# Local/global attention and a hard-swish layer on one core: all steps in a new written order

## The chip, the cores and the metric

The kernel runs on one core of a Trainium2 chip. The core has five instruction queues that run beside each other and wait for one another only through semaphores: TensorE (PE, with its weight loads PEld), VectorE (DVE), ScalarE (ACT), GpSimd (POOL) and SyncE (SP). SP issues most of the DMAs, POOL issues some. The metric is the device time of one execution in microseconds (us): 318.76 us is the median of three runs (317.52 to 319.28). A lower time is better.

## The reference

For each of 8 batches and 8 heads there are 512 local positions and 32 global ones, with a head size of 64. A global query attends to all 544 keys. A local query attends to the 32 global keys and to the local keys at a distance of at most 32. The result, 4352 rows of 512, goes through two dense layers with a hard-swish between them:

```
s_g  = scale * q_g @ [k_g, k_l].T ;  out_g = softmax(s_g) @ [v_g, v_l]
s_l  = scale * [q_l @ k_g.T, where(|i-j| <= 32, q_l @ k_l.T, -1e9)]
out_l = softmax(s_l) @ [v_g, v_l]
x = concat(out_g, out_l) per batch, heads side by side      # 4352 x 512
h = x @ w_in                                                # 512 -> 2048
y = (h * clip(h + 3, 0, 6) / 6) @ w_out                     # 2048 -> 512
```

## The kernel before

The kernel is straight-line: every step is a token in one long string, `ORDER`, and `run` calls a small function for each token. `pin` then chains the instructions of each engine (and the DMA issues of SP and POOL) in that written order. So the string fixes, for each of the five queues, which instruction stands behind which. It doesn't fix when one starts: that is set by the queue ahead of it and by the semaphores. A second string, `SEATS`, names for each tile that a token takes which physical buffer ("seat") it gets: 7 banks of PSUM (`ps`), 13 staging buffers for loads (`stg`), 3 or 4 buffers of each kind for the rest.

Work goes by pairs of heads, numbered p = 4 * batch + m, so 32 pairs in 8 batches, four pairs to a batch. The tokens that matter here, with the argument after the dot and often an engine letter at the end (v = VectorE, a = ScalarE, g = GpSimd, s = SyncE):

- `ld.p.c` loads k, q or v of a pair into a staging buffer (256 KB, on SP's queue); `lw.i.n` and `lw.o.n` load 16 blocks each of w_in and w_out the same way.
- `ca.p.c.e` casts a staged k, q or v to 16 bits; `cw.i.n.e` and `cw.o.n.e` cast a weight block. All casts and most copies go through the helper `copy`, L132.
- `Tp` and `Te` transpose a k or q on TensorE and copy it out of PSUM; `Td` does the same by a DMA transpose on SP's queue instead. `qw` copies 32 columns of a transposed q (the wrap of the window). `kg`, `vg`, `vG` and `vs` put the global keys and values and a shifted copy of the values beside the local ones.
- `Sp.p.ch` computes half of a pair's scores (8 half-height matmuls of 128 columns: four windows for each of two PSUM tiles), `Se` is the exponential on ScalarE (L295). The mask of the window is put in one of two ways: `Sm.p.ch` writes it into the PSUM tiles ahead of the scores by two matmuls of 512 columns (L273), or `Sv` multiplies the exponentials by zeros and ones on VectorE (L299).
- `Ap` multiplies the exponentials with the values (L332, L335), `An` divides by the row sum on VectorE (L344, L345), `Qp`, `Qe`, `Pp`, `Ga` and `Gv` do the global queries.
- `Xd` transposes a pair's result for the dense layers by DMA, `Xp` and `Xe` do it on TensorE with a copy.
- `Hp.f.c.m0.m1` are matmuls of the first dense layer for batch f and hidden block c (L409; f = 8 is the 256 global rows), `Ha` and `Hv` the hard-swish on ScalarE (L414) and VectorE (L420); `Hv` is also what frees the PSUM seat.
- `Op.f.t.c4` are four of the 16 matmuls of an output tile (L428), `Oe` copies it out, `Os` stores it from SP's or POOL's queue (L445).

Batches overlap by the written order: while TensorE does the second dense layer of one batch, the attention of the next is put in between in short bursts of scores. The first batch is special: nothing can fill TensorE until loads, casts and transposes of pairs 0 to 3 are through, and the w_in blocks arrive behind them.

Of the kernel before, what the change touches and what calls it, by code (L numbers as in the profile page):

```python
# [14 lines left out]
def kernel(  # L15
# [40 lines left out]
ps 00123456012341653064120645132054321506324062615302421206545230542654452541255146206153461236140236142305121050  # L56
25613024354613410320613456143562416451325434512034510264640621350432015042630631543265152431605431654321036456
01452301052164103461042563124561256130135650124564305216340252150421362530652433254625416520264351052463050216
531456405162351064326346365102345620562021564032351065624620316053405616341652314502601432650134065234514210 ;
stg 0123456789abc0123456798bc12304a65798c1b3042a65798c1b3042a657981cb3042a67c8594b302a617c89b4103265c7a489132056a4  # L60
b19728c3b46157cab349527 ;
kn 01230213021302103201233103230120 ;
qn 01230213021321302130123120313120 ;
qT 01231023102312302132103210232002 ;
E 01210210210210210210210201210210 ;
xn 01201201201202102102102102120121 ;
t1 01230120132103210321023103120312032130120120132013201321032103102310231203201320132013201323013202310231023102
1302130213012301231023102310231032 ;
ot 0123120132313213130013030122210202
# [10 lines left out]
    def const(name, shape, dtype=FP16):  # L80
        return constp.tile(shape, dtype, tag=name, name=name)
# [12 lines left out]
    vg = const("vg", [P, B, H, D])  # L94
# [423 lines left out]
iv id ig fg.1.v im fv.1.v ov.0.0 ov.0.1 ld.0.k lg.k.0 ca.0.k.a wm.7 Gc.k.0.a Gp.k.0 ld.0.q lv.0 Tp.0.k ld.1.q fv.0.v  # L518
ov.1.0 ov.0.2 ca.0.q.v Tp.0.q fk.0 Te.0.q.v Ge.k.0.a kg.0.v ld.1.k ld.2.q Te.0.k.a qw.0.v ld.2.k ld.3.k ld.2.v ld.3.q
ca.2.q.v fg.0.g ca.1.q.g Tp.1.q Te.1.q.a ca.2.k.a ca.1.k.g Tp.1.k qw.1.g Te.1.k.v vg.0.2.v Sp.0.1 Sp.1.0 Se.1.0.1 ik  # L520
Se.0.1.1 vg.0.0.v Sv.0.1.1 lw.i.6 ld.0.v ld.1.v Se.0.1.0 lw.i.5 Sp.1.1 lw.i.4 ld.3.v lw.i.0 lw.i.2 lw.i.7 lw.i.1
lw.i.11 lw.i.3 Se.1.1.1 lw.i.8 lw.i.10 vg.0.1.v ca.3.k.g lw.i.9 ld.4.q lw.i.12 lw.i.14 lg.k.1 lw.i.13 lw.i.15 lw.o.2
ld.4.k ld.5.q lw.o.0 lw.o.1 Tp.2.q Tp.2.k Se.1.0.0 Tp.3.k Te.2.q.a Te.2.k.a lw.o.3 Te.3.k.v lg.q.0 Sm.2.1 ca.2.v.v
ca.3.q.g qw.2.v Se.1.1.0 vs.2.v vg.0.3.v ca.1.v.g ca.0.v.v vs.0.g vs.1.g cw.i.4.g Sm.0.0 Sp.0.0 Se.0.0.0 Sp.2.1 Tp.3.q
Se.0.0.1 Sm.2.0 Sp.2.0 Sm.3.0 Se.2.1.0 Se.2.0.0 Se.2.1.1 ca.3.v.g Se.2.0.1 Sv.0.1.0 Sv.1.1.0 Te.3.q.v qw.3.v Sp.3.0
Ap.0.1 Ap.0.0 Se.3.0.0 ov.0.3 Sm.3.1 Sp.3.1 Sv.1.1.1 Sv.1.0.0 Sv.1.0.1 An.0.0 An.0.1 Ap.1.0 Ap.1.1 Se.3.1.1 fe.3
Se.3.1.0 An.1.0 Xp.0 Xe.0.a An.1.1 Ap.2.1 Ap.2.0 Xp.1 Se.3.0.1 Hp.0.4.0.1 An.2.0 An.2.1 Xe.1.a cw.i.0.g vs.3.g
Hp.0.5.0.1 fe.0 cw.i.5.a Ap.3.1 An.3.1 Ap.3.0 Hp.0.0.0.1 cw.i.2.a Xp.2 Hp.0.4.1.2 Hp.0.6.1.2 An.3.0 cw.i.11.g cw.i.6.v
Hp.0.2.0.1 Xe.2.a ca.4.q.g cw.i.1.v Xp.3 Hp.0.6.0.1 Gc.k.1.g Hp.0.0.2.3 Hp.0.4.2.3 Hp.0.5.1.2 Hp.0.0.1.2 cw.i.7.v
Hp.0.1.2.3 Xe.3.v Hp.0.4.3.4 Hp.0.6.2.3 Hp.0.5.2.3 Hp.0.5.3.4 Hp.0.8.3.4 ov.1.1 ov.1.2 cw.i.3.v Hp.0.2.3.4 Hp.0.0.3.4  # L530
Hp.0.2.2.3 Hp.0.6.3.4 qz Ha.0.4 cw.i.13.g Hp.0.2.1.2 Hp.0.1.3.4 Ha.0.5 Ha.0.0 Ha.0.6 cw.i.12.g Ha.0.2 Hp.0.1.1.2
Hp.0.3.1.2 vG.0.v Hv.0.4 Hp.0.1.0.1 cw.i.8.v Hp.0.3.2.3 Hp.0.8.0.1 Hp.0.3.0.1 Hp.0.7.0.1 Hv.0.5 cw.i.10.a cw.i.15.g
Hv.0.0 Ha.0.1 cw.i.9.v cw.o.2.g ca.4.k.g ca.5.q.g Hp.0.3.3.4 cw.o.0.g lw.o.4 lw.o.6 lw.o.5 Hp.0.8.1.2 lw.o.7
Hp.0.7.3.4 Hp.0.10.3.4 Hp.0.11.0.1 Hp.0.11.2.3 cw.o.1.g Hp.0.11.3.4 Tp.4.q lv.1 cw.o.3.g Hp.0.8.2.3 Hp.0.10.1.2
Hp.0.9.2.3 Hp.0.9.0.1 Hv.0.2 Ha.0.3 Hp.0.7.1.2 cw.i.14.a Gp.k.1 Hp.0.11.1.2 Hp.0.13.2.3 Hp.0.10.2.3 Hp.0.9.3.4
Hp.0.7.2.3 Hp.0.9.1.2 Hp.0.12.0.1 Te.4.q.a Ha.0.8 Hp.0.12.3.4 Ha.0.11 Ha.0.7 Hv.0.1 Hv.0.6 Hv.0.3 lw.o.10 Hp.0.12.2.3
Hp.0.12.1.2 Hp.0.13.1.2 Hp.0.14.1.2 Hp.0.13.0.1 Hp.0.14.2.3 Hp.0.15.2.3 Ge.k.1.v kg.1.a Hv.0.11 Hv.0.8 Hv.0.7 qw.4.v
Ha.0.9 Hp.0.10.0.1 Hp.0.14.0.1 Hp.0.15.1.2 Tp.4.k Ha.0.12 Ha.0.10 Hp.0.14.3.4 Te.4.k.a fk.1 Hp.0.15.0.1 Tp.5.q Hv.0.9
Ha.0.14 Hp.0.15.3.4 Hp.0.13.3.4 Sp.4.1 fe.2 lw.o.9 ld.5.k lw.o.8 lw.o.11 Op.0.2.0 fe.1 ld.6.q Op.0.0.0 Hv.0.12 Hv.0.10
Hv.0.14 lw.o.12 lw.o.14 lw.o.13 lw.o.15 ld.4.v Gc.q.0.g cw.o.6.g cw.o.5.g Gp.q.0 ld.6.k ld.5.v ld.7.q Se.4.1.0 ld.7.k  # L540
ld.6.v Ha.0.15 Te.5.q.v ca.6.q.g Se.4.1.1 cw.o.4.a qw.5.v Hv.0.15 Ge.q.0.v cw.o.7.v Sv.4.1.0 Sp.4.0 Op.0.1.0 ca.5.k.v
Ha.0.13 Sv.4.1.1 cw.o.8.v cw.o.12.g Qp.1 Qp.2 Op.0.0.1 cw.o.11.v Se.4.0.0 Qe.2 Op.0.2.1 Qe.1 Pp.1 Qp.0 Op.0.1.1 Qp.3
cw.o.10.a Sv.4.0.0 Tp.5.k cw.o.9.a Se.4.0.1 Qe.3 Qe.0 ov.1.3 Te.5.k.a Pp.2 Op.0.1.2 Hv.0.13 Op.0.2.2 Tp.6.q cw.o.13.a
vg.1.0.g Op.0.0.2 Sp.5.1 Te.6.q.v Sp.5.0 Se.5.0.1 Sv.4.0.1 vg.1.2.v cw.o.15.v Pp.0 Pp.3 vg.1.3.v cw.o.14.g vg.1.1.a
Sv.5.0.1 Op.0.1.3 ca.6.k.g lv.5 ca.4.v.v vs.4.v Op.0.0.3 qw.6.g Qp.5 Ap.4.0 ca.5.v.g Se.5.1.1 Oe.0.1.v Ap.4.1 Se.5.1.0
Se.5.0.0 Oe.0.0.a Tp.6.k Te.6.k.a Op.0.2.3 Sp.6.1 Sp.6.0 Qe.5 ld.8.k Sv.5.1.0 Oe.0.2.a Sv.5.0.0 An.4.0 Sv.5.1.1 An.4.1
vs.5.v vG.1.v Se.6.0.0 Sv.6.0.0 ca.7.q.g Se.6.0.1 Op.0.3.2 Ap.5.1 ca.7.k.g Ap.5.0 Tp.7.q Tp.7.k An.5.1 Se.6.1.0
Sv.6.1.0 Te.7.q.a An.5.0 Op.0.3.0 Xp.4 qw.7.g ca.6.v.g vs.6.g ld.7.v ld.9.k ld.8.q lv.3 Te.7.k.a ld.11.k ld.11.q
ld.9.v Sv.6.0.1 ca.7.v.g ld.10.k Sp.7.0 Sp.7.1 Op.0.3.1 Se.6.1.1 Xe.4.v Se.7.0.0 Se.7.0.1 Sv.6.1.1 ld.9.q Ap.6.1
Ap.6.0 Se.7.1.0 Se.7.1.1 Xp.5 Op.0.3.3 Sv.7.0.0 ld.10.q Sv.7.0.1 Hp.1.2.0.1 An.6.0 Xe.5.a ld.11.v ld.8.v An.6.1  # L550
Sv.7.1.0 Qp.6 Hp.1.5.1.2 vs.7.g Sv.7.1.1 kg.2.v Oe.0.3.a Xp.6 Hp.1.12.0.1 Qe.6 Ga.0 Qp.4 Xe.6.v Ap.7.1 Ap.7.0 An.7.0
An.7.1 Qe.4 Hp.1.9.1.2 ca.11.q.g Hp.1.5.0.1 lv.2 ca.8.q.a ca.8.k.a ca.9.k.g Td.8.k Gv.0 Hp.1.2.2.3 Hp.1.9.0.1
Hp.1.9.2.3 Hp.1.0.2.3 Hp.1.0.1.2 Xp.7 Hp.1.4.0.1 Xe.7.v Hp.1.2.1.2 Hp.1.0.0.1 Hp.1.4.1.2 Hp.1.9.3.4 Ha.1.9 Hp.1.2.3.4
Hp.1.0.3.4 Hp.1.3.2.3 Hp.1.4.2.3 Hp.1.4.3.4 Hv.1.9 Ha.1.2 Ha.1.4 Hv.1.4 Hp.1.12.2.3 Hp.1.12.3.4 Hp.1.3.0.1 Hp.1.1.2.3
Hp.1.5.2.3 Hp.1.12.1.2 Ha.1.0 Ha.1.12 Hp.1.1.1.2 Hp.1.3.1.2 Hp.1.5.3.4 ca.10.q.g Hp.1.1.3.4 Hp.1.3.3.4 Hp.1.1.0.1
Hp.1.8.3.4 Hp.1.8.0.1 Hp.1.8.2.3 Hv.1.2 Hp.1.13.2.3 Hp.1.7.0.1 Hp.1.7.2.3 Pp.4 Hp.1.8.1.2 Ha.1.5 Ha.1.3 Ha.1.1 Hv.1.0
ca.9.q.a Hv.1.12 ca.9.v.g Tp.8.q Hp.1.7.3.4 Hp.1.6.2.3 Hp.1.10.1.2 ld.12.k Hp.1.13.3.4 Hp.1.6.0.1 Hp.1.13.0.1 Hv.1.3
Ha.1.8 Hv.1.1 ca.10.k.g Te.8.q.a Hv.1.5 Hp.1.13.1.2 vg.2.3.a vg.2.1.g Hv.1.8 Pp.5 Ha.1.13 Hp.1.7.1.2 Hv.1.13 Qp.7 Qe.7
Ha.1.7 Hp.1.15.1.2 Hp.1.15.3.4 Hp.1.15.0.1 Hp.1.15.2.3 Hp.1.11.2.3 Hp.1.10.3.4 Hv.1.7 Hp.1.6.1.2 Tp.9.k Ha.1.15
Hv.1.15 Te.9.k.v ld.12.q qw.8.g Hp.1.10.2.3 ca.11.v.g Td.10.q Hp.1.6.3.4 Hp.1.10.0.1 Hp.1.14.3.4 Hp.1.11.0.1 Os.0.0.g  # L560
ca.8.v.v Ha.1.6 Tp.10.k Ha.1.10 Hp.1.11.1.2 Qp.8 Pp.7 Hp.1.14.0.1 ca.12.k.v Te.10.k.a vg.3.0.g vG.2.g Hv.1.6 Qe.8
Hp.1.11.3.4 Hp.1.14.2.3 Hp.1.14.1.2 Sp.8.1 Ha.1.11 Sp.8.0 Ha.1.14 Se.8.0.0 Se.8.1.1 ld.13.k Se.8.0.1 Op.1.0.0 Td.9.q
ld.13.q Td.11.q Hv.1.10 Hv.1.14 Op.1.0.1 Op.1.3.3 ca.12.q.v Tp.12.q vs.8.g Os.0.2.s ld.12.v qw.9.v Se.8.1.0 vg.2.2.g
vs.9.g qw.10.g Op.1.0.3 Pp.6 Sp.9.1 Sp.9.0 Hv.1.11 ca.11.k.g ca.13.k.a Td.11.k Sv.8.0.0 Sv.8.0.1 Te.12.q.a vg.2.0.v
Sv.8.1.0 Sv.8.1.1 kg.3.g vs.11.v ca.13.q.v Op.1.0.2 Ap.8.0 qw.12.v qw.11.g Se.9.1.0 Sv.9.1.0 Qp.10 Se.9.0.0 Se.9.1.1
Ap.8.1 An.8.0 An.8.1 Se.9.0.1 Sv.9.0.1 Op.1.3.1 ld.15.q Sp.11.1 Sp.11.0 Sp.10.0 Oe.1.0.a Op.1.3.2 Qe.10 Se.11.0.0
Sv.9.0.0 Td.12.k vg.3.3.v Sv.9.1.1 Ga.1 lg.k.4 ld.10.v Td.13.k Td.13.q Se.10.0.0 Sv.10.0.0 Op.1.2.3 Op.1.2.0 ca.15.q.g
# [153 lines left out]
```

## Time and profile before

| what | value |
|---|---|
| time, median of 3 runs | 318.76 us |
| the profiled execution's own time | 319.3 us |
| its span, first to last instruction | 317.5 us |
| mean granted TensorE clock | 0.987 of full speed |
| busy: PE, DVE, ACT, POOL | 304.4, 228.7, 224.7, 87.2 us |
| read from and written to main memory | 35.13 MB, 8.91 MB |

"Busy" is the time in which at least one instruction of the engine was under way. Busy time of TensorE close to the span means that it is hardly ever without an instruction; it doesn't say in itself that each of them ran at full speed, so the granted clock is read beside it. The views used are the page, the busy time by stretches of the span (windows), the waits, the groups of instructions and the timeline.

### The profile page before, as it was taken

What the parts mean: (1) busy time and instruction counts of PE and PEld (TensorE: products, weight loads), DVE (VectorE), ACT (ScalarE), POOL (GpSimd) and SP (SyncE); (2) the same over time, 40 slices, a digit from 0 to 9 for tenths busy, and PEclk for the clock granted to TensorE, in tenths of its full rate; (3) what the DMA queues carried; (4) which work ended last, traced back from release to release, by engine and by line L of the source; (5) the groups of instructions that cost most, each with busy time, mean ns of one, the idle gap of its engine ahead of it and who ended that gap; (6) DMA issues with size and microseconds to landing.
All of it is one profiled execution on the core that took longest, in us unless ns stands there. A gap on an engine that the chain in (4) does not pass through costs nothing.

```text
span 317.5 us, 7441 instructions
## 1 busy us (share of the span) xinstructions
PE 304.4 (96%) x2781; PEld 162.2 (51%) x2781; DVE 228.7 (72%) x550; ACT 224.7 (71%) x446; POOL 87.2 (27%) x160
## 2 busy tenths in 40 slices
PE   5888999989999999999999999999999999999995
PEld 1553555645555455445555555545544565455442
DVE  7898797977897799298847996499736894276320
ACT  6789787979897878677749986697639871566201
POOL 6263734633430442162540404251200000000010
PEclk9599999999999999999999999999999999999999
DMA  7999999977679997999999999870940016020024
GB/s 214 285 327 298 298 360 267 215 144 151 124 173 207 204 225 167 184 244 192 224 171 214 204 204 211 183 168 18 151 100 2 0 25 144 33 92 11 0 76 157
DMA packets 138661, 52.93 MB, mean 167 GB/s; under 512 B 127168, under 2 KB 131264, under 8 KB 138624
## 3 DMA queue, kind: packets, MB, share of 16 engines
q1 hardware_dynamic: 135008, 47.73, 67.8%
q0 software_dynamic: 3616, 4.72, 6.1%
q8 instruction: 22, 0.36, 0.4%
q14 instruction: 15, 0.12, 0.1%
HBM read 35.13 MB, written 8.91 MB: 139 GB/s over the span
## 4 chain that ended last, share of the span: by engine, by line
PE 75%; DVE 18%; ACT 3%; issue 1%; DMA 1%; SPq 0%; DVEq 0%
PE po L428 32%; PE psH L409 30%; DVE E L299 4%; PE psS L285 4%; DVE gt L420 4%; DVE xn L345 2%; PE pav L332 2%; PE pg L359 2%; PE pav L335 2%; DVE vb L132 1%; PE psSG L309 1%; DMA xt<-xn 1%; DVE qT L132 1%; ACT E L295 1%; DVE win L132 1%
## 5 line engine op out<-in xcount | busy, mean ns | idle before, releaser
L428 PE MATMUL po<-wout,gt 128*128 128x512 f16 x544 | 130.9, 379 | 0.2
L409 PE MATMUL psH<-xt,win 128*128 128x512 f16 x512 | 126.3, 379 | 2.1 <-DVE win L132 1.3
L420 DVE SCALAR_TENSOR_TENSOR gt<-t,psH 128x512 f16<-128x512 f32 (+1 forms) x144 | 89.4, 653 | 36.0 <-ACT t L414 32.0
L414 ACT ACTIVATE t<-psH,half_col 128x512 f32<-128x512 f32 (+1 forms) x144 | 89.5, 663 | 34.2 <-PE psH L409 32.3
L409 PEld LDWEIGHTS <-win 128*128 128x128 f16 x576 | 53.4, 98 | 54.1 <-DVE win L132 1.8
L295 ACT ACTIVATE E<-psS 128x512 f16<-128x512 f32 x128 | 67.8, 604 | 14.4 <-PE psS L285 13.4
L428 PEld LDWEIGHTS <-gt 128*128 128x128 f16 x544 | 49.1, 97 | 51.3 <-issue 0.4
L299 DVE TENSOR_TENSOR E<-E,mk 128x512 f16<-128x512 f16 x118 | 52.3, 471 | 5.0 <-ACT E L295 4.4
L445 POOL DMA_DIRECT2D out_dram<-ot x22 | 11.8, 538 | 75.7 <-DVE ot L132 70.0
L132 ACT COPY ot<-po 128x512 f32<-128x512 f32 x18 | 10.6, 591 | 26.7 <-PE po L428 26.7
L345 DVE TENSOR_TENSOR xn<-pav,rc 128x256 f16<-128x256 f32 x64 | 27.2, 425 | 2.2
L132 DVE COPY ot<-po 128x512 f32<-128x512 f32 x16 | 10.9, 688 | 18.1 <-PE po L428 14.2
L132 POOL CAST qn<-stg 128x512 f16<-128x512 f32 x18 | 11.6, 647 | 44.1 <-DMA stg<-in_q_l_dram 40.6
L335 PE MATMUL pav<-vb,E 128*128 128x65 f16 x256 | 22.5, 194 | 0.7 <-DVE E L299 0.6
L285 PE MATMUL psS<-qT,kT 64*128 64x128 f16 x512 | 21.6, 224 | 1.7 <-DVE qT L132 1.4
L332 PE MATMUL pav<-vt,E 128*128 128x65 f16 x256 | 22.6, 193 | 0.0
L285 PEld LDWEIGHTS <-kT 64*128 64x128 f16 x512 | 15.4, 97 | 13.8 <-issue 8.6
L332 PEld LDWEIGHTS <-E 128*128 128x128 f16 x256 | 18.8, 98 | 4.3 <-issue 0.2
L335 PEld LDWEIGHTS <-E 128*128 128x128 f16 x256 | 17.6, 97 | 4.4 <-DVE E L299 0.7
L132 POOL COPY qT<-qT 128x32 f16<-128x32 f16 x18 | 4.6, 261 | 41.6 <-DMA qT<-qn 23.4
L132 POOL COPY vb<-vt 64x512 f16<-64x512 f16 x15 | 9.9, 666 | 19.0 <-DVE vt L132 9.2
L313 ACT ACTIVATE Eg<-psSG 128x256 f16<-128x256 f32 x32 | 12.5, 389 | 3.1 <-PE psSG L309 2.9
(95 smaller groups left out, 274.3 us busy)
## 6 DMA issues: line engine op xcount, KB each, us to landing
stg<-in_k_l_dram SPq DMA_DIRECT2D x32, 256.0 KB, 4.2
stg<-in_q_l_dram SPq DMA_DIRECT2D x32, 256.0 KB, 3.9
stg<-in_v_l_dram SPq DMA_DIRECT2D x32, 256.0 KB, 4.0
stg<-in_moe_w_in_dram SPq DMA_DIRECT2D x16, 256.0 KB, 6.2
stg<-in_moe_w_out_dram SPq DMA_DIRECT2D x16, 256.0 KB, 4.5
out_dram<-ot SPq DMA_DIRECT2D x12, 256.0 KB, 2.3
out_dram<-ot POOLq DMA_DIRECT2D x12, 256.0 KB, 3.2
out_dram<-ot POOLq DMA_DIRECT2D x5, 192.0 KB, 3.3
```

The costliest lines, as they stand in the source:

```text
L132: (nc.scalar.copy if eng == "a" else ENG[eng].tensor_copy)(out=out, in_=in_)
L285: nc.tensor.matmul(out=st[p, ch][e][:, w * P:(w + 1) * P], lhsT=kT[r, c0:c0 + P], rhs=qT[r, w * P:(w + 1) * P], start=not added, stop=True ...
L295: nc.scalar.activation(out=E_of(p)[:, ch, e], in_=st[p, ch][e], func=EXP, scale=qk_scale)
L299: nc.vector.tensor_tensor(out=E[:, ch, e], in0=E[:, ch, e], in1=mk[:, ch].rearrange("p w c -> p (w c)"), op=mult)
L313: nc.scalar.activation(out=Eg[:, 0:NT].rearrange("p u e s -> p (u e s)"), in_=ps[:, 0:NT * 2 * Sg], func=EXP, scale=qk_scale)
L332: nc.tensor.matmul(out=o, lhsT=E[:, 0, e, w * P:(w + 1) * P], rhs=vt[:, w, h, 0:D + 1], start=True, stop=False, skip_group_check=True)
L335: nc.tensor.matmul(out=o, lhsT=E[:, 1, e, w * P:(w + 1) * P], rhs=vb[:, (w - 1) % NT, h, 0:D + 1], start=False, stop=True, skip_group_chec ...
L345: nc.vector.tensor_tensor(out=st[p, "xn"][:, 2 * w2:2 * w2 + 2].rearrange("p w (e d) -> p w e d", e=2), in0=pv[:, :, :, 0:D], in1=rc.to_br ...
L409: nc.tensor.matmul(out=st["H", f, c][:, 0:FN(f)], lhsT=w_in_t[m][:, c * P:(c + 1) * P], rhs=x, start=(k == 1), stop=(k == NM), skip_group_ ...
L414: nc.scalar.activation(out=t1[:, 0:FN(f)], in_=st["H", f, c][:, 0:FN(f)], func=RELU, bias=half_col, scale=1.0 / 6.0)
L420: nc.vector.scalar_tensor_tensor(out=gts[f, c][:, 0:n], in0=st["t", f, c][:, 0:n], scalar=1.0, in1=st["H", f, c][:, 0:n], op0=amin, op1=mult)
L428: nc.tensor.matmul(out=st["O", f, t][:, 0:dm], lhsT=gts[f, c][:, t * P:(t + 1) * P], rhs=w_out_t[c // 4][:, c % 4], start=(k == 1), stop=( ...
```

## The change

All 2170 tokens of `ORDER` become 2167 in another order, and `SEATS` is written anew to fit it. No function is changed. What the new string has otherwise, by counting tokens:

| tokens | before | after |
|---|---|---|
| casts (`ca`, `cw`) on POOL / DVE / ACT | 65 / 36 / 27 | 74 / 29 / 25 |
| mask by matmul `Sm` / by multiply `Sv` | 5 / 118 | 7 / 114 |
| transposes of k and q: `Tp` / `Td` | 21 / 43 | 20 / 44 |
| stores `Os` from POOL / from SP | 17 / 17 | 26 / 8 |
| `vs` on POOL / DVE / ACT | 15 / 13 / 4 | 17 / 7 / 8 |
| runs of `Sp` in a row on TensorE's queue | 33 | 35 |

The first loads change places (before: k of pair 0, a part of k_g, q of pair 0, q of pair 1; after: k of pair 1, k of pair 0, q of pair 0, the part of k_g, q of pair 1), and pair 1 gets its mask by matmul. In both strings six matmuls of the first dense layer stand ahead of the fourth pair's `Xp`. The start and the end of the string, cut:

```diff
-iv id ig fg.1.v im fv.1.v ov.0.0 ov.0.1 ld.0.k lg.k.0 ca.0.k.a wm.7 Gc.k.0.a Gp.k.0 ld.0.q lv.0 Tp.0.k ld.1.q fv.0.v
-ov.1.0 ov.0.2 ca.0.q.v Tp.0.q fk.0 Te.0.q.v Ge.k.0.a kg.0.v ld.1.k ld.2.q Te.0.k.a qw.0.v ld.2.k ld.3.k ld.2.v ld.3.q
...
+fg.1.v iv fv.0.v id ld.1.k ld.0.k ld.0.q fg.0.g lg.k.0 ld.1.q ov.0.0 ov.0.1 ov.0.2 ca.0.q.a ca.1.k.a wm.7 Tp.0.q
+ld.2.q ld.3.q fv.1.v ca.1.q.a ig lv.0 Te.0.q.a im ca.0.k.v Gc.k.0.g Sm.0.0 lw.i.1 ld.0.v Tp.0.k Gp.k.0 Tp.1.q Sm.1.1
+ld.2.k ld.3.k qw.0.g ik fk.0 Tp.1.k ld.3.v ld.1.v Te.0.k.a Te.1.q.v qw.1.g ca.2.q.g vg.0.1.g ca.3.k.g Te.1.k.v Sp.0.0
...
+Hp.0.5.2.3 cw.i.12.g Hp.0.0.3.4 Hp.0.0.0.1 cw.i.8.v Hp.0.2.3.4 Hp.0.0.2.3 cw.i.13.g Ha.0.4 Hv.0.4 Ha.0.3 Hv.0.3 Ha.0.1
+Hv.0.1 Gc.k.1.g ca.5.q.g cw.i.10.a fe.1 cw.i.11.a ca.4.k.g cw.o.1.g Hp.0.7.3.4 cw.i.9.v Ha.0.0 lg.q.0 lw.o.6 lw.o.5
+ov.1.1 lw.o.4 lw.o.7 Hp.0.7.1.2 Hv.0.6 Hp.0.11.2.3 Hp.0.2.0.1 Hp.0.7.2.3 ld.5.k lw.o.9 Ha.0.5 Hp.0.2.1.2 Hp.0.2.2.3
...
-Oe.7.0.a Op.8.0.3 Oe.8.0.v Op.7.2.2 Op.7.3.0 Op.7.2.1 Os.6.1.s Os.6.0.s Op.7.3.1 Os.8.0.s Op.7.2.0 Oe.7.2.a Os.8.1.s
-Op.7.3.2 Os.7.2.s Os.7.1.g Os.5.3.s Os.7.0.g Op.7.3.3 Oe.7.3.a Os.7.3.s
...
+Op.8.1.3 Op.8.0.3 Op.8.1.0 Os.6.2.g Os.5.0.s Os.6.3.g Os.7.0.s Os.6.1.g Oe.8.0.a Os.8.0.s Oe.7.1.v Oe.8.1.v Op.7.3.1
+Op.7.3.2 Op.7.3.3 Oe.7.3.a Os.7.3.s Os.7.1.g Os.8.1.g
```

## The prediction

> **What bounds the kernel now.** I read the page first, for the engines' shares:
>
> ```profile
> span 317.5 us, 7441 instructions
> ...
> PE 304.4 (96%) x2781; PEld 162.2 (51%) x2781; DVE 228.7 (72%) x550; ACT 224.7 (71%) x446; POOL 87.2 (27%) x160
> ...
> PEclk9599999999999999999999999999999999999999
> ```
>
> TensorE has an instruction under way in 96% of the span, at full clock in all but the second of 40 slices. Only 317.5 - 304.4 = 13.1 us are idle. The next view, the busy time by stretches, says where. I cut it at the last exponential of the first batch (22.42 us), at the first matmul of the second dense layer (39.83) and at 70 and 240 us; the columns are the stretch, its length, then PE, PEld, DVE, ACT, POOL busy and the granted clock:
>
> ```profile
> 0.00:9.50 9.50, 4.90 (x30) 2.17 (x32) 7.09 (x22) 6.08 (x11) 5.36 (x15) 0.97 0.83 233
> 9.50:22.42 12.92, 11.34 (x147) 6.99 (x148) 11.69 (x31) 10.56 (x21) 6.41 (x11) 0.76 1.04 295
> 22.42:39.83 17.41, 16.14 (x112) 7.91 (x111) 14.75 (x35) 15.24 (x27) 9.52 (x16) 1.00 0.99 306
> 39.83:70.00 30.17, 28.98 (x329) 16.74 (x326) 25.48 (x60) 25.21 (x55) 13.63 (x23) 1.00 1.02 245
> 70.00:240.00 170.00, 169.41 (x1639) 89.82 (x1637) 131.27 (x321) 130.12 (x260) 50.69 (x94) 1.00 0.89 176
> 240.00:317.50 77.50, 73.60 (x535) 38.54 (x534) 38.44 (x86) 37.49 (x76) 1.56 (x3) 0.99 0.20 55
> ```
>
> Of the idle time 4.6 us lie ahead of 9.5 us, 1.58 by 22.42, 1.27 by 39.83, 1.19 by 70; then 0.59 in 170 us, and 3.9 at the end. From 70 us on there is nothing to win by order: it can only be lost there. What an order can win lies ahead of 70 us, at most the 4.0 us after 9.5 us, and part of the start. TensorE's waits name the releasers:
>
> ```profile
> PE psTq L247 <- DVE qn L132: 2.4, 1, 2.4
> PE psS L285 <- DVE qT L132: 1.4, 2, 0.8
> PE psH L409 <- DVE win L132: 1.3, 1, 1.3
> PE psW L498 <- DVE ones L455: 1.2, 1, 1.2
> PE pav L335 <- DVE E L299: 0.6, 1, 0.6
> PE psH L409 <- DVE xt L132: 0.4, 1, 0.4
> ```
>
> All are VectorE. Ahead of 66 us it is nearly always busy, and some of its instructions are long (columns: busy, mean ns, idle before):
>
> ```profile
> L299 DVE TENSOR_TENSOR E<-E,mk 128x512 f16<-128x512 f16 x22 | 12.3, 580 | 0.8 <-ACT E L295 0.8
> ...
> L132 DVE CAST win<-stg 128x512 f16<-128x512 f32 x6 | 4.0, 699 | 0.0
> ```
>
> The mask multiply takes 580 ns here. The 1.3 us wait for w_in has its cause on the timeline:
>
> ```profile
> 29.28 2.10 DVE L132 CAST win<-stg 128x512 f16<-128x512 f32 x1
> ```
> ```profile
> 29.37 1.73 POOL L132 CAST win<-stg 128x512 f16<-128x512 f32 x3
> ```
>
> One VectorE cast lasts 2.10 us while GpSimd does three casts at 0.58 us each; the other five share 4.0 - 2.1, 0.38 each. VectorE is held by GpSimd.
>
> **The change part by part.** Work per queue is counted in the two strings, each token at a row's mean.
>
> *TensorE.* Two more `Sm` are four matmuls of 512 columns, one `Tp` less four of 128. The end of the span gives the pace:
>
> ```profile
> 298.01 15.70 PE L428 MATMUL po<-wout,gt 128*128 128x512 f16 x72
> ```
>
> That is 0.218 us each, so +0.87 us, and a quarter of it back for each transpose matmul, -0.22. The +0.87 falls into the first batch and is in the next sum.
>
> *The start, up to the first `Op`.* The rows of before:
>
> ```profile
> 3.55 0.62 ACT L132 CAST kn<-stg 128x512 f16<-128x512 f32 x1 [0.40 <-DMA stg<-in_k_l_dram]
> ```
> ```profile
> 6.38 0.61 POOL L132 CAST qn<-stg 128x512 f16<-128x512 f32 x1 [1.54 <-DMA stg<-in_q_l_dram]
> ```
> ```profile
> 11.01 2.56 ACT L295 ACTIVATE E<-psS 128x512 f16<-128x512 f32 x5 [1.28 <-PE psS L285]
> ...
> 21.82 0.60 ACT L295 ACTIVATE E<-psS 128x512 f16<-128x512 f32 x1
> ```
> ```profile
> 39.83 1.90 PE L428 MATMUL po<-wout,gt 128*128 128x512 f16 x8
> ```
>
> The first load has landed at 3.55, the fourth (q of pair 1) at 6.38. In the new string q of pair 0 is the third: about 5.8 by interpolation. ScalarE casts it (0.62), k and q of pair 1 follow on the same queue (to about 7.6), then `Te.0.q` to 8.2. The masks are late on VectorE, since both fills stand ahead of them: about 7.6. TensorE then does `Sm.0.0`, `Tp.0.k`, `Tp.1.q`, `Sm.1.1`, `Tp.1.k`, at half clock to about 10.7, `Sp.0.0` to 11.3. So the first exponential starts at about 11.35, 0.34 later than before. From there ScalarE's queue has 16 exponentials and only `ov.0.3`, `ca.1.v`, `Te.3.k` between them. At 0.51 (2.56 / 5) and 0.6 for the three, 10.0 us: the last one ends at 21.4, where before it was 22.42 with the idle 2.4 us of its stretch (12.92 - 10.56). Then `Xe.1`, `cw.i.6`, `Xe.2`, `cw.i.2` at 0.6: 23.8, and TensorE's stream runs from about 24.1, `Xp.3` and six `Hp` done. Left up to the first `Op` are 58 `Hp` and five short tokens, 58 x 0.218 + 1.2 = 13.8: 37.9. `Te.4.k` stands behind 13 `Ha` and a memset on ScalarE; I add 0.5: 38.4. Last, `cw.i.9.v` comes on VectorE where GpSimd has `cw.i.12` and `cw.i.13`: between nothing and the 1.3 us wait of before, and I take 0.6, as only two GpSimd casts meet it where there were three. 39.0 against 39.83: **-0.8 us** (-1.4 to +0.5; the top is a start 1.3 late). That agrees with the queues: ahead of the last `Ha` of the first batch ScalarE has four instructions of 0.6 fewer, ahead of the last `Hv` VectorE has seven mask multiplies and five weight casts fewer, 7 x 0.58 + 5 x 0.70 = 7.6 us, which were its surplus.
>
> *The second batch's attention (39.83 to 70).* Ahead of the last `An.7` VectorE's queue has 4 mask multiplies and 2 weight casts fewer in all (3.7 us), ScalarE's ahead of the last `Se.7` one instruction fewer (0.6), TensorE's 0.9 us more, counted above. TensorE idled 1.19 us here, 1.0 of it in the two last waits of the list, both for VectorE. With 3.7 us off that queue I let them go: **-1.1** (-1.2 to +1.0, if ScalarE is late in VectorE's place: its queue is 25.21 busy of 30.17).
>
> *From 70 to 240.* In sum VectorE loses some 6 us, GpSimd gains 9 casts and 9 stores, 9 x 0.6 + 9 x 0.54:
>
> ```profile
> L445 POOL DMA_DIRECT2D out_dram<-ot x22 | 11.8, 538 | 75.7 <-DVE ot L132 70.0 <-ACT ot L132 5.2 <-issue 0.5
> ```
>
> Both have room: 131 and 51 of 170 us. The distances on TensorE's queue between the last `Ap` of a pair and its first `Hp`, which must cover `An` and the transpose, are at least 4 us of matmuls in both strings from batch 2 on. The 0.22 for the transposes comes back, and one or two new waits of the size of the old (0.4) are likely: **+0.1** (-0.6 to +3).
>
> *Stores and the end.* How long a store takes from either queue:
>
> ```profile
> out_dram<-ot SPq DMA_DIRECT2D x12, 256.0 KB, 2.3
> out_dram<-ot POOLq DMA_DIRECT2D x12, 256.0 KB, 3.2
> ```
> ```profile
> 313.75 0.58 ACT L132 COPY ot<-po 128x512 f32<-128x512 f32 x1 [1.10 <-PE po L428]
> ```
>
> The moved stores land 0.9 us later, hidden while three other `ot` buffers are free. At the end `Os.7.3` stays on SP: 317.5 - 313.75 = 3.75 us from its copy. `Os.8.1.g` issues four pieces of 0.54 behind a copy done about 1.8 us before TensorE's end: +0.4, and 3.2 to land, +3.6. The same end: **0** (to +0.6).
>
> Sum: -0.8 - 1.1 + 0.1 = -1.8 us. The profiled execution took 319.3 us, 0.5 above the median of the runs; so 317.5 in its terms, 317.0 against 318.76.
>
> **The rule that speaks against it.** Row first: 2.10 us for a cast that else takes 0.38. The Trainium skill, "SBUF — State Buffer", section "SBUF: two separate sides", calls the port pair that GpSimd and VectorE share an exclusive lock, held for the whole instruction, and the trace agrees (2.10 beside three casts of 0.58). By that rule alone each of the nine more GpSimd casts could hold VectorE for its 0.6 us, 5.4 us in sum on its queue, and the second rival below would be the forecast.
>
> **The rivals.**
> 1. *The order changes nothing that counts* (within 0.5%). TensorE's work grows by 0.65 us and the start is set by loads that land when they did. For it: DMA share about 1.0 through the first 70 us. Against: the waits of the list are for VectorE. The start gives 0 and the second batch -0.5: 318.3 to 318.9.
> 2. *VectorE held beside GpSimd at the wrong places* (slower). `cw.i.8`, `cw.i.9`, `cw.i.14` stand beside a chain of GpSimd casts; a hold delays all `Hv` behind it, and with them the PSUM seats. Held as in the row above, each costs TensorE the 1.3 us wait of then; three are 3.9 on a start of -1.4 without any, +2.5, and a VectorE that late doesn't let the second batch's waits go: +2.6 with the 0.1 of the middle, 321.4. It decides with the third hold; with two the start is +1.2, still no measurable loss.
> 3. *A store behind a late transfer on GpSimd's queue* (slower).
>
> ```profile
> POOL qn L132 <- DMA stg<-in_q_l_dram: 40.6, 8, 11.3
> ```
> ```profile
> DVE ot L132 <- DMA out_dram<-ot: 3.8, 2, 2.8
> ```
>
> GpSimd stood up to 11.3 us at one cast whose load was late. Each store behind such a cast keeps an `ot` buffer; the next `Oe` on VectorE waits, as it did twice (2.8 at most), and `Hv` behind it. With nine stores more in that queue, two such waits in a row on TensorE's path give 2 x 2.8 - 1.8 = +3.8: 322.6. Against it: so far these waits cost TensorE nothing. It decides once a wait outlasts TensorE's lead over `Hv`, some 2 us.
>
> **How the numbers follow.** Two executions of this kernel differ by up to 0.5%, 1.6 us; less can't be told from no change. The forecast has 0.46 (314.5 to 317.2), the first rival 0.24, the second 0.18, the third 0.12. The low end, 314.5, takes the lower bounds of all three sums (-1.4 - 1.2 - 0.6) and 1 us of the 1.58 idle between 9.5 and 22.42. The high end, 321.8, takes in the second rival and a little of the third's spread, and leaves out most of the third.
>
> **What would show it.** Right: the first `Op` at about 39.0; the last exponential of the first batch ending at 21.4; no wait of TensorE for `E` or `xt` between 50 and 70 us; TensorE idle under 1 us from 70 to 240. Wrong: a VectorE cast of w_in over 1 us with TensorE waiting for `win`; a first `Op` after 41; `ot` waiting for stores with TensorE idle behind it; or idle time of over 2 us in the middle, for a releaser that isn't in the list above.

## The result, and the profile after

The changed kernel takes 317.28 us (median of 22 runs, 315.7 to 321.56), the kernel before 318.51 in the same comparison (22 runs, 317.38 to 321.7): 0.9954 of its time, 95% interval 0.9938 to 0.997. That is 1.5 us less by the ratio, inside the forecast's range and 0.3 us from its number. The interval excludes 1, but the 0.46% is small: it is less than the 0.5% by which, the prediction says, two executions of the same kernel can differ. A second measurement gave 0.9967 (0.9939 to 0.9995).

The page of the profiled execution (316.41 us, 0.9 below the median of its runs, where the one of before was 0.8 above its own, so the two profiles differ by more than the kernels do):

```profile
span 314.6 us, 7441 instructions
...
PE 303.6 (97%) x2781; PEld 161.9 (51%) x2781; DVE 219.9 (70%) x531; ACT 225.6 (72%) x447; POOL 99.5 (32%) x185
```

VectorE is busy for 8.8 us less, GpSimd for 12.3 more. The same stretches as in the prediction; columns: stretch, length, PE, PEld, DVE, ACT, POOL busy, granted clock, DMA share, GB/s:

```profile
0.00:9.50 9.50, 6.18 (x27) 2.85 (x28) 5.83 (x20) 6.16 (x11) 4.48 (x14) 1.00 0.77 208
9.50:22.42 12.92, 10.88 (x153) 6.83 (x151) 10.06 (x27) 9.87 (x21) 8.11 (x14) 0.87 0.90 255
22.42:39.83 17.41, 17.26 (x119) 8.76 (x118) 14.79 (x34) 16.45 (x30) 10.20 (x17) 1.00 1.07 324
39.83:70.00 30.17, 30.10 (x335) 17.22 (x333) 22.99 (x61) 27.30 (x59) 13.81 (x25) 1.00 1.02 253
70.00:240.00 170.00, 169.38 (x1655) 89.58 (x1653) 129.62 (x315) 131.48 (x262) 57.18 (x105) 1.00 0.94 180
240.00:314.60 74.60, 69.82 (x501) 36.65 (x499) 36.63 (x80) 34.36 (x69) 5.75 (x11) 1.00 0.17 52
```

TensorE's idle time, length less PE: 3.32 us ahead of 9.5 (before 4.6), 2.04 by 22.42 (1.58), 0.15 by 39.83 (1.27), 0.07 by 70 (1.19), 0.62 by 240 (0.59), 4.78 at the end (3.9). The gain lies between 22 and 70 us, 2.24 us in two stretches that now have almost no idle time; 0.88 of it is given back at the end. Ahead of 22 us TensorE idles 0.82 us less as well, but that bought nothing: the last exponential of the first batch ends no earlier (22.55 against 22.42). The waits of TensorE that are left:

```profile
PE psW L498 <- DVE ones L455: 2.5, 1, 2.5
PE psTk L247 <- DVE kn L132: 2.0, 1, 2.0
PE psTq L247 <- ACT qn L132: 0.8, 1, 0.8
PE pav L335 <- DVE E L299: 0.5, 1, 0.5
```

The waits for `win` and `xt` are gone, and the one for `E` has moved to 86.63 us. New is a wait of 2.0 us for `kn`, and the timeline shows what it is: k of pair 2 landed at 13.5 us, and its transpose could not start before.

```profile
10.99 1.09 ACT L295 ACTIVATE E<-psS 128x512 f16<-128x512 f32 x2 [1.17 <-PE psS L285]
...
13.50 0.43 DVE L132 CAST kn<-stg 128x512 f16<-128x512 f32 x1 [0.43 <-DMA stg<-in_k_l_dram]
13.98 0.40 PE L247 MATMUL psTk<-ident,kn 128*128 128x128 f16 x4 [2.04 <-DVE kn L132]
...
18.49 4.06 ACT L295 ACTIVATE E<-psS 128x512 f16<-128x512 f32 x8 [0.38 <-PE psS L285]
...
24.81 10.55 PE L409 MATMUL psH<-xt,win 128*128 128x512 f16 x48
...
29.73 0.39 DVE L132 CAST win<-stg 128x512 f16<-128x512 f32 x1
...
38.63 1.89 PE L428 MATMUL po<-wout,gt 128*128 128x512 f16 x8
```

The first exponential starts at 10.99, the last ends at 22.55 (18.49 + 4.06). From 24.81 on 48 matmuls of the first dense layer run without a gap, block 9 of w_in is cast in 0.39 us (2.10 before), and the second layer starts at 38.63 (39.83 before; 39.34 in the profile of the second measurement). The other end, and then the closing `DRAIN` of GpSimd's queue, in the changed kernel and in before:

```profile
308.25 2.01 POOL L445 DMA_DIRECT2D out_dram<-ot  x4 [2.05 <-DVE ot L132]
309.86 0.58 ACT L132 COPY ot<-po 128x512 f32<-128x512 f32 x1 [2.87 <-PE po L428]
```
```profile
L716 POOLq DRAIN  x3: 46/102/4215, 309.6 to 314.3; - x3
```
```profile
L716 POOLq DRAIN  x3: 46/102/4426, 305.6 to 317.3; - x3
```

The last two fences give of three drains the shortest, median and longest in ns, then the first and the last start; the longest is the first one. From the start of the last copy to the end of the span it is 314.6 - 309.86 = 4.74 us, where it was 3.75. GpSimd's closing drain starts at 309.6, behind its last store in the queue, and lasts 4.2 us: it is over at 313.8, while the last packet of GpSimd's stores had landed at 311.3. In before it was over at 310.0, ahead of the last copy.

### The profile page after: what moved, and what is told of

It is laid out like the page before. It is cut to its first block, busy times and chain, and to the rows that moved or that the text cites. A ratio compares the mean times of both kernels' runs of the same rounds, so it can differ in the third digit from the quotient of the medians.

```text
span 314.6 us, 7441 instructions
## 1 busy us (share of the span) xinstructions
PE 303.6 (97%) x2781; PEld 161.9 (51%) x2781; DVE 219.9 (70%) x531; ACT 225.6 (72%) x447; POOL 99.5 (32%) x185
## 4 chain that ended last, share of the span: by engine, by line
PE 84%; ACT 7%; DMA 3%; DVE 2%; issue 1%; SPq 1%; ACTq 0%
PE po L428 35%; PE psH L409 34%; PE psS L285 5%; DMA stg<-in_k_l_dram 3%; ACT E L295 2%; PE pav L335 2%; PE pav L332 2%; ACT t L414 2%; PE pg L359 2%; PE psSG L309 1%; DVE E L299 1%; DVE gt L420 1%; SPq L144 1%; PE psS L273 1%; ACT Eg L313 1%
## 5 line engine op out<-in xcount | busy, mean ns | idle before, releaser
L409 PE MATMUL psH<-xt,win 128*128 128x512 f16 x512 | 122.6, 379 | 0.0
L409 PEld LDWEIGHTS <-win 128*128 128x128 f16 x576 | 54.2, 98 | 54.1 <-ACT win L132 0.3
L295 ACT ACTIVATE E<-psS 128x512 f16<-128x512 f32 x128 | 67.9, 607 | 15.0 <-PE psS L285 13.8
L299 DVE TENSOR_TENSOR E<-E,mk 128x512 f16<-128x512 f16 x114 | 49.4, 464 | 10.0 <-ACT E L295 9.3
L445 POOL DMA_DIRECT2D out_dram<-ot x34 | 18.1, 535 | 79.9 <-ACT ot L132 57.8
L132 DVE COPY ot<-po 128x512 f32<-128x512 f32 x17 | 11.6, 688 | 16.8 <-PE po L428 16.5
L285 PEld LDWEIGHTS <-kT 64*128 64x128 f16 x512 | 14.9, 96 | 12.3 <-issue 9.0
L132 POOL CAST vt<-stg 128x512 f16<-128x512 f32 x19 | 12.5, 661 | 26.7 <-DMA stg<-in_v_l_dram 26.6
L132 POOL CAST qn<-stg 128x512 f16<-128x512 f32 x21 | 13.3, 636 | 23.4 <-DMA stg<-in_q_l_dram 19.4
L132 POOL COPY vb<-vt 64x512 f16<-64x512 f16 x17 | 10.9, 648 | 20.9 <-DVE vt L132 11.1
```

The source lines that it names most:

```text
L132: (nc.scalar.copy if eng == "a" else ENG[eng].tensor_copy)(out=out, in_=in_)
L285: nc.tensor.matmul(out=st[p, ch][e][:, w * P:(w + 1) * P], lhsT=kT[r, c0:c0 + P], rhs=qT[r, w * P:(w + 1) * P], start=not added, stop=True ...
L295: nc.scalar.activation(out=E_of(p)[:, ch, e], in_=st[p, ch][e], func=EXP, scale=qk_scale)
L299: nc.vector.tensor_tensor(out=E[:, ch, e], in0=E[:, ch, e], in1=mk[:, ch].rearrange("p w c -> p (w c)"), op=mult)
L409: nc.tensor.matmul(out=st["H", f, c][:, 0:FN(f)], lhsT=w_in_t[m][:, c * P:(c + 1) * P], rhs=x, start=(k == 1), stop=(k == NM), skip_group_ ...
L445: q.dma_start(out=out[at:at + nr, :], in_=st["ot", f, t][r0:r0 + nr, :])
```

## The experiments

The seat strings follow the written order in each of them.

| kernel | median us | ratio to before, 95% |
|---|---|---|
| changed kernel again | 317.43 | 0.9967 (0.9939 to 0.9995) |
| its last store on SP | 316.05 | 0.9932 (0.9903 to 0.9961) |
| its k loads earlier | 315.50 | 0.9895 (0.9861 to 0.9929) |
| 12 of its stores on SP | 317.27 | 0.9960 (0.9940 to 0.9979) |
| its casts on the engines of before | 347.51 | 1.0912 (1.0859 to 1.0964) |
| its pair 1 masked by multiplies | 321.77 | 1.0095 (1.0064 to 1.0125) |
| its wait for k filled | 316.89 | 0.9953 (0.9927 to 0.9979) |
| before, one cast on ScalarE | 319.52 | 1.0016 (0.9993 to 1.0040) |
| before, pair 1 masked by matmuls | 318.05 | 0.9974 (0.9950 to 0.9998) |
| before, its wait for q filled | 317.72 | 0.9979 (0.9953 to 1.0004) |
| changed, k loads and last store | 314.67 | 0.9887 (0.9852 to 0.9922) |

The first four ran on one chip, the other comparisons on two more; medians of before there were 318.49 to 318.78.

**The changed kernel again.**

> The changed kernel once more, as it is, beside the kernels that each differ from it in one thing. Its first measurement gave 0.9954 (0.9938 to 0.997) of the time before; both theories expect the same here, 1.0 to 1.9 us under the kernel before. A value outside of that would say that the gain itself varies from chip to chip.

It came out at -1.1 us by the median, -0.3% by the ratio; the two intervals overlap.

**The late load of k.**

```diff
-ld.2.q ld.3.q fv.1.v ca.1.q.a ...
+ld.2.q ld.2.k ld.3.q ld.3.k fv.1.v ca.1.q.a ...
...
-ld.2.k ld.3.k qw.0.g ik ...
+qw.0.g ik ...
```

> The changed kernel with two loads earlier on SP's queue: k of pair 2 right behind q of pair 2, k of pair 3 right behind q of pair 3 (in the changed kernel both stand further behind, and k of pair 2 landed at 13.5 us, with TensorE waiting 2.04 us for its cast). Theory: the late load is why the last exponential of the first batch ended at 22.55 us and not at the forecast 21.4; here the 2.0 us wait goes, the exponentials end at 21.0 to 21.6, the first matmul of the second dense layer starts at 37.6 to 38.3 (38.63), and the time falls by 0.4 to 1.0 us. Rival: the loads are bound by bytes, so what comes earlier makes something else later (v, then the blocks of w_in), the wait shows under another name, the first matmul of the second layer starts at 38.4 to 39.0, and the time is that of the changed kernel within 0.3 us.

1.9 us less than the changed kernel beside it, and the intervals don't overlap: the theory, with twice its price. The timeline of this kernel:

```profile
11.21 0.42 DVE L132 CAST kn<-stg 128x512 f16<-128x512 f32 x1
...
15.61 4.02 ACT L295 ACTIVATE E<-psS 128x512 f16<-128x512 f32 x8
...
23.63 0.43 DVE L132 CAST win<-stg 128x512 f16<-128x512 f32 x1 [1.46 <-DMA stg<-in_moe_w_in_dram]
...
37.47 1.90 PE L428 MATMUL po<-wout,gt 128*128 128x512 f16 x8
```

k of pair 2 is cast 2.3 us earlier, the last exponential ends at 19.63, 2.9 us earlier, and the first matmul of the second layer comes 1.2 us earlier. In this execution the rival is right for what lies beyond: VectorE now waits 1.46 us for a block of w_in, and more than half of the lead is gone by 37 us. A part of the 2.9 us is the clock, though (last section): TensorE runs at full rate from 5.1 us here, in the profile of the changed kernel from 11.0. The kernel with both gains below has the same early loads and full rate from 11.0 too; there the exponentials end at 21.6 and the second layer starts at 37.76, both 0.9 us earlier than in the changed kernel, and VectorE doesn't wait for w_in. So some 0.9 of the 1.9 us are located; where the rest is gained stays open.

**The end.**

```diff
-... Oe.7.1.v Oe.8.1.v Op.7.3.1 Op.7.3.2 Op.7.3.3 Oe.7.3.a Os.7.3.s Os.7.1.g Os.8.1.g
+... Oe.7.1.v Oe.8.1.v Os.8.1.s Op.7.3.1 Op.7.3.2 Op.7.3.3 Oe.7.3.a Os.7.3.s Os.7.1.g
```

> The changed kernel with one store moved: the store of block 8, piece 1 goes from GpSimd's queue to SP's, right behind its eviction. Theory: GpSimd's closing DRAIN (4.2 us, behind its last store) sets the end of the changed kernel; without that store GpSimd is done earlier, the drain is hidden, and from the last copy to the end it takes 3.75 us again as before, where it was 4.74: 0.7 to 1.0 us less than the changed kernel, 2.2 to 2.5 less than the kernel before. Rival: the last transfer's landing sets the end and the drain only fills the time; then the end stays within 0.2 us of 4.74 and the time is that of the changed kernel.

```profile
301.22 9.95 SPq L445 DMA_DIRECT2D out_dram<-ot  x11
...
309.94 0.58 ACT L132 COPY ot<-po 128x512 f32<-128x512 f32 x1 [2.87 <-PE po L428]
```
```profile
L716 POOLq DRAIN  x3: 46/102/3922, 305.7 to 313.7; - x3
```

GpSimd's drain now starts at 305.7 and is over at 309.6, ahead of the last copy; the end takes 314.0 - 309.94 = 4.06 us instead of 4.74. So the drain set the end, and 0.7 us of the 1.0 lost there come back; the rest doesn't, as SP now issues 11 pieces up to 311.2. The medians say 1.4 us, but the ratios' intervals overlap: only the 0.7 of the trace is shown.

**The other stores.** Twelve tokens `Os` of the changed kernel get the letter s for g:

```diff
-Os.0.2.g Os.1.0.g Os.3.2.g ... Os.6.2.g Os.6.3.g Os.6.1.g Os.8.1.g
+Os.0.2.s Os.1.0.s Os.3.2.s ... Os.6.2.s Os.6.3.s Os.6.1.s Os.8.1.s
```

> The changed kernel with 12 of its 20 stores on GpSimd's queue moved to SP's queue (as many as before had on each side, roughly). If the move of stores to GpSimd cost nothing but the end (theory): 0.7 to 1.0 us less than the changed kernel, all of it behind the last copy, and the stretch from 70 to 240 us the same within 0.2 us of TensorE idle time. If the stores on GpSimd's queue are part of the gain (rival: SP's queue stood behind stores that wait, and loads behind them came late): 0.5 to 2 us more between 70 and 300 us, with waits of an engine for a transfer of q, k or w_out, which eat the gain at the end or more.

```profile
302.35 11.57 SPq L445 DMA_DIRECT2D out_dram<-ot  x12
...
311.07 0.58 ACT L132 COPY ot<-po 128x512 f32<-128x512 f32 x1 [2.87 <-PE po L428]
```

Neither came. Between 70 and 240 us TensorE idles 0.26 us, so the queue of the stores costs nothing in the middle, as the theory had it. But the end takes 316.6 - 311.07 = 5.53 us: SP still issues pieces until 313.92, 2.3 us after the last copy is done. `Os.8.1` now stands behind `Os.7.3` in SP's queue, so its four pieces wait for the last copy, although their own data had been ready since 309.2. The time is that of the changed kernel.

**The casts' engines.** 64 tokens `ca` and `cw` get their letter of before, the sequence stays:

```diff
-ca.0.q.a ca.1.k.a ca.1.q.a ca.0.k.v ... cw.i.11.a cw.i.14.v ...
+ca.0.q.v ca.1.k.g ca.1.q.g ca.0.k.a ... cw.i.11.g cw.i.14.a ...
```

> The changed kernel's order, with every cast of an input and of a weight on the engine that it had before (64 casts change engine; masks, loads, stores and the sequence stay). Theory A, the order of the steps and the masks bring the gain: the time stays within 0.5 us of the changed kernel. Theory B, the gain is that VectorE is relieved and no longer held beside GpSimd: VectorE's casts of w_in go back to a mean of 0.6 to 0.7 us (0.51 now), a wait of TensorE for a w_in or xt of 0.4 to 2 us comes back, and the time is 1 to 3 us more than the changed kernel, so that of the kernel before or worse.

Waits of TensorE in this kernel:

```profile
PE psH L409 <- DVE gt L420: 10.4, 3, 7.5
PE psH L409 <- POOL win L132: 3.6, 1, 3.6
```

29 us more than before, far outside of both. Whole queues stand still (one wait of 7.5 us for `gt`), while VectorE's casts of w_in have a mean of 527 ns, short of the 0.6 to 0.7 us of theory B (511 in the changed kernel). So this doesn't tell A from B. What it shows is that sequence and engines can't be had apart: a cast on another engine stands behind other instructions there.

**The mask of pair 1, in both kernels.** In the changed kernel `Sm.1.0` and `Sm.1.1` go and four `Sv.1` come behind their exponentials; in the kernel before it is the other way round.

```diff
-... Tp.1.q Sm.1.1 ... Sm.1.0 ...
+... Tp.1.q ... Sv.1.1.0 ... Sv.1.1.1 ... Sv.1.0.0 ... Sv.1.0.1 ...
```

> The changed kernel with the masks of pair 1 applied by four VectorE multiplies, as before, in place of two mask matmuls (four instructions of 512 columns) on TensorE. Theory: the mask matmuls run in TensorE time that is idle anyhow (3.3 us ahead of 9.5 us), and the four multiplies cost VectorE 4 x 0.44 = 1.8 us ahead of the second product of pair 1; so without the mask matmuls the first exponential is no more than 0.3 us earlier, TensorE waits 0.3 to 1.0 us for E, and the time is 0 to 0.8 us more than the changed kernel. Rival: the forecast's +0.87 us of TensorE work is paid in full, VectorE has room for the multiplies; then the time is 0.5 to 0.9 us less than the changed kernel.

```diff
-... Sv.0.1.0 Sv.1.1.0 ... Sv.1.1.1 Sv.1.0.0 Sv.1.0.1 ...
+... Sp.0.1 Sm.1.0 ... lw.i.5 Sm.1.1 ... Sv.0.1.0 ...
```

> The kernel before with the masks of pair 1 put on by two mask matmuls on TensorE in place of four VectorE multiplies (four of the 22 multiplies ahead of 66 us, 0.58 each, 2.3 us). Theory: VectorE's queue is what the first batch waits for; the wait for qT or for w_in shortens, and the time falls by 0.3 to 1.0 us although TensorE gets 0.87 us more to do. Rival: TensorE's 0.87 is paid and the VectorE time isn't on the path: 0.3 to 0.9 us more than the kernel before.

The second has the sign and size of its theory, 0.8 us less by the ratio, but its interval only just excludes 1. Its profile can't say that the masks did it: block 9 of w_in isn't held there either (0.42 us), and that changes between executions, as the clock's experiment shows. The first has the right sign and five times the size, 4.3 us more than the changed kernel. Its waits:

```profile
PE pav L335 <- DVE E L299: 2.3, 1, 2.3
PE psS L273 <- DVE qT L132: 1.5, 1, 1.5
...
PE psH L409 <- DVE win L132: 0.9, 1, 0.9
```

The four multiplies make VectorE late; TensorE waits for `E`, `qT` and then `win`, its clock is halved from 17.78 to 24.61 us, around the wait of 2.3, and the second layer starts at 43.37. All of the loss is ahead of that: from there to the end of the span it takes 275.7 us, in the changed kernel 276.0.

**The held VectorE cast of before.**

```diff
-... Ha.0.1 cw.i.9.v cw.o.2.g ...
+... Ha.0.1 cw.i.9.a cw.o.2.g ...
```

> The kernel before with a single cast moved: block 9 of w_in is cast by ScalarE instead of VectorE, so the VectorE cast that was held for 2.10 us beside three GpSimd casts isn't there. Theory of the prediction: TensorE's wait of 1.3 us for this block goes, the first matmul of the second layer starts at 38.5 to 38.9 (39.83), and the time falls by 0.6 to 1.3 us. Rival: the wait is only one of several that would end late there, the next block or the gate is late next; the time stays within 0.3 us of the kernel before, with a wait of over 0.8 us under another name.

```profile
31.23 1.47 PE L409 MATMUL psH<-xt,win 128*128 128x512 f16 x6 [0.95 <-ACT win L132]
```

The rival: the held cast is gone, and TensorE waits 0.95 us for the same block from ScalarE, where it was 1.26 from VectorE. The time is that of before.

**The clock.** `wm` is a run of warm-up matmuls, results unused.

```diff
-... lv.0 Tp.0.k ld.1.q ...
+... lv.0 Tp.0.k wm.9 ld.1.q ...
```

> The kernel before with nine more of its warm-up matmuls on TensorE (9 x 0.216 us at full clock, results unused), behind the transpose of k of pair 0, where TensorE waits 2.4 us for q of pair 0. In the profile of before the granted clock fell to 0.5 from 8.93 to 15.76 us, right after that wait; where TensorE was kept busy (the kernel before with two mask matmuls, its profile) it stayed at 1.0. Theory, part of the loss at the start is this half clock: with the wait filled the granted clock is 1.00 in all of the first 40 us, the last exponential ends 0.3 to 1.0 us earlier (22.42), and the time falls by 0.4 to 1.5 us. Rival: TensorE at half clock is still ahead of the loads and of ScalarE's exponentials there, so the clock costs nothing: the time stays within 0.3 us of the kernel before.

```diff
-... Tp.2.k ...
+... wm.8 Tp.2.k ...
```

> The changed kernel with eight more warm-up matmuls (8 x 0.216 us) on TensorE in front of the transpose of k of pair 2, where it waits 2.04 us for that load's cast and where the granted clock then fell to 0.5 from 14.45 to 17.86 us in the profile (12.03 to 18.85 in the second one). Theory, half clock costs time: the granted clock stays at 1.00, the last exponential ends at 21.4 to 22.0 us (22.55 with one such window, 23.2 with two), and the time falls by 0.5 to 1.2 us though the load is as late as before. Rival: only the late load counts and the clock nothing; then the time is that of the changed kernel, or up to 0.5 us more where the load comes earlier than in the profile and the matmuls stand in the way.

The second diff is the changed kernel's. In both the recorded clock stays at 1.00 in the first 40 us, and the last exponential ends at 22.32 (22.42 without; less than expected) and at 21.23 (22.55). The times are 0.8 and 0.4 us lower by the medians, and neither can be told from its own kernel without the filling: before's interval just includes 1, and the changed kernel's is the same as its first, 0.9954. So what that half clock costs stays open: from nothing to 1.5 us by the interval of before's run. One ground given for the theory was wrong besides: before with two mask matmuls was not kept at full clock, its matmuls run at half rate up to 13.5 us (the last section tells how that is seen).

Why the held cast of before is no steady cost is seen here too. The same stretch in the profile of before, and then in that of the kernel with the filled wait:

```profile
28.81 0.61 POOL L132 CAST kgn<-stg 96x512 f16<-96x512 f32 x1 [2.03 <-DMA stg<-in_k_g_dram]
```
```profile
28.47 0.61 POOL L132 CAST kgn<-stg 96x512 f16<-96x512 f32 x1 [2.61 <-DMA stg<-in_k_g_dram]
29.18 0.42 DVE L132 CAST win<-stg 128x512 f16<-128x512 f32 x1
```

In before GpSimd's cast of k_g runs from 28.81 to 29.42, VectorE's cast begins at 29.28 and is held until the three casts behind are through as well. Here it ended at 29.08, 0.1 us ahead of VectorE's cast, which took 0.42; TensorE had no wait for `win`, and the second layer started at 38.31. A landing 0.3 us earlier decides over 1.3 us.

**Both gains together.** The edits of the late load and of the end in one kernel.

> The changed kernel with both of the edits that helped: k of pairs 2 and 3 loaded right behind their q, and the store of block 8, piece 1 on SP's queue. Theory, the two are independent (one acts ahead of 22 us, the other behind the last matmul): their gains add, 0.9895 and about -0.7 us give 314.5 to 315.2 us, 3.3 to 4.0 us under the kernel before. Rival: the earlier start is given back later, or both gain by the same thing; then it is no better than the kernel with the two loads alone (315.5, ratio 0.9895).

314.67 us, in the expected range, 3.8 us under before: first exponential 11.13, second layer from 37.76, end 312.6 - 308.61 = 3.99 us. By its ratio, 0.9887, it beats the changed kernel (0.9954); against the kernel with the loads alone (0.9895) the difference can't be told.

## Why the prediction was right, and where not

- **The second batch, -1.1.** TensorE's idle time between 39.83 and 70 us went from 1.19 to 0.07: -1.12, and the waits for `E` and `xt` are gone. This part is steady: the four profiles with before's order, or one edit of it, have 1.1 to 2.0 us there, the eight of the changed kernel and its edits (without the casts' one) 0.07 to 0.44. But the reason given, 3.7 us fewer on VectorE ahead of the last `An.7`, isn't it. All of those multiplies and casts stand ahead of the first `Op`, and in before VectorE had caught up by then:

```profile
49.29 0.69 DVE L132 COPY qT<-psTq 128x512 f16<-128x512 f16 x1 [1.61 <-PE psTq L247]
```

  It waits 1.61 us for TensorE just ahead of the stretch with the waits. And the four multiplies, 2.3 of the 3.7 us, were moved one way and the other; before without them, then the changed kernel with them:

```profile
39.83:70.00 30.17, 28.80 (x326) 16.67 (x324) 24.41 (x60) 25.43 (x55) 13.90 (x24) 1.00 1.13 264
```
```profile
39.83:70.00 30.17, 30.06 (x352) 17.66 (x351) 22.98 (x62) 27.20 (x59) 15.13 (x26) 1.00 1.04 265
```

  TensorE idles 1.37 and 0.11 us, so these multiplies aren't what made the waits go. What the new order does is to relieve VectorE in the stretch itself: from 50 to 66 us it is busy for 12.83 of 16 us, in before for 15.44. Which of the moved steps does it, no run tells. That the number fits is in part luck. **From 70 to 240, +0.1:** 0.59 became 0.62.
- **The start, -0.8 on the first `Op`.** -1.2 in one profile, -0.5 in the other, both against a single profile of before in which block 9 was held; without the hold, in the kernel with the filled wait, that string came to 38.31. So how much of it is steady isn't shown. The sum (39.0) comes out near 38.63 and 39.34, but two of its terms do not hold, and they cancel, which is luck. The last exponential was put at 21.4 with ScalarE's queue taken as never waiting; it ended at 22.55, since k of pair 2 had become the late one (21.6 with both gains, where that load is earlier). The prediction costed the queues of ScalarE and VectorE but took only the first four loads from rows, and k of pair 2 is the seventh load of k or q in the new string. So TensorE's stream starts at 24.81 and not at 24.1. Against it stand two allowances that weren't needed, 0.5 for `Te.4.k` and 0.6 for a hold of block 9: 24.81 and the counted 13.8 us of matmuls are 38.6.
- **The mask matmuls, +0.87 as a price.** Their work was counted right; what they spare was put at seven multiplies of surplus on VectorE. Taking those of pair 1 out costs 4.3 us, nearly three times the whole gain: this string stands on them, where the string of before got 0.8 us from the same masks, hardly clear of noise.
- **The end, 0 to +0.6.** +1.0. The working asked when the bytes of `Os.8.1.g` land (they did in time) and not what GpSimd does after its last store. The last-store kernel puts the mis-sized term at 0.7.
- **Sum.** The profiles differ by 2.9 us of span, 2.15 of it idle time; the medians by 1.2 and 1.1, the ratios by 1.5 and 1.1. The forecast of 1.8 is a little too much, by 0.3 to 0.7 us; the end's miss (0.7 to 1.0) would account for that.
- **The rivals.** That the order changes nothing fails by its mechanism (the start and the second batch did gain), though by size the result lies in its band. VectorE held at `cw.i.8`, `cw.i.9` and `cw.i.14` didn't come (0.39 to 0.43 us); it does come in the kernel with multiplies, where `cw.i.14` took 2.36 us. Stores behind late transfers cost nothing: twelve of them moved back to SP changed the middle by 0.4 us of idle time at most.
- **The rule on the shared port pair.** It would have cost 5.4 us by itself. The traces bear out the lock (2.10 and 2.36 us, where such a cast alone takes 0.42), but two things decide what it costs. It is met where a GpSimd cast is already under way: only one of the changed kernel's four casts of w_in on VectorE was longer than 0.5 us (0.80, begun 0.1 us into a GpSimd cast). And once met it lasted longer than that one instruction: VectorE got through only when all of the GpSimd casts in a row were done, four of them both times (counting the one under way).

## What to carry to other kernels

When a written order is judged, walk every queue, the load queue too: the engines' queues alone gave the sum, but hid the 1.9 us that earlier loads of two k gave, the cheapest gain in this study. A count of work per queue says little across a point where that queue has caught up; look first whether it idles in between. An instruction moved onto the bottleneck engine can be the best part of a change if that engine is idle there anyway and the relieved engine is the late one; a part's worth is only known inside its own order. A wait that hangs on a phase of 0.1 us is a chance, not a cost: ask which of two engines comes first, and look at a second execution before pricing it.

## What the hardware showed

The granted clock in the profile's rows is 1.00 until its first record, and that is not so. Two mask matmuls of 512 columns in the changed kernel, then in the kernel with the earlier loads, both at a granted 1.00:

```profile
6.89 1.06 PE L273 MATMUL psS<-mneg,ident 128*128 128x512 f16 x2
```
```profile
6.94 0.59 PE L273 MATMUL psS<-mneg,ident 128*128 128x512 f16 x2
```

By the distances of such matmuls (427 ns or 216) TensorE runs at half rate from its first matmul to the first clock record, which came at 5.1 us in the kernel with the earlier loads, at 11.0 in the changed kernel, and at 13.5 in before with two mask matmuls.

After it, the changes of the clock lie whole multiples of 3.41 us apart in all 13 profiles. Cut into windows of that length from the first record to the last matmul, TensorE's records show when full rate is lost: nine full-rate windows had 1.73 us or more of idle time, about half of the window, and each of them is followed by half rate; none of the other 1131, with 1.69 us at most, is. In the changed kernel the window is 11.04 to 14.45 (2.05 idle, the wait for `kn`), and half rate lasts to 17.86; in before it is 5.52 to 8.93 (2.52 idle, the wait for `qn`), and half rate lasts for two windows, to 15.76. It ended only behind a window with 0.08 us of idle time or less; one with 0.54 was not enough. So the same wait costs the clock or not, depending on how the windows cut it.

The Trainium skill, "TensorE: Matmul & The Clock Gate", section "Part 1: The HAM clock gate (the "warmup" mystery)", has windows of 3413 ns that run free of the kernel's start; the trace agrees with both, as the first record came at 11.0 and 5.2 us in two executions of the changed kernel. The spread that the page gives for this point, 500 ns to either side, is far exceeded here. So the clock of the first 20 us differs from one execution to the next, and two profiles of the same kernel differ there (by 0.7 us at the first `Op`) by more than most edits.

GpSimd's closing drain behind stores that it issued takes 3.5 to 4.4 us (before 4.43, changed kernel 4.22, with twelve stores moved 3.45); in the changed kernel that was 2.5 us past the landing of the last packet. Where GpSimd's last store is early enough, as in before, the drain is hidden behind TensorE; where it is among the last of the kernel, the drain sets the end.
